# Moving a negated table to ScalarE, GpSimd's index work to the end of its queue, and splitting the last batch of inverse roots

## The chip, the cores and the metric

The kernel runs on one core of one Trainium2 chip. Its time is the device time of one execution in microseconds (us). Five engines work side by side, each in the order of its own queue: PE (TensorE, matrix products), DVE (VectorE), ACT (ScalarE), POOL (GpSimd), and SP (SyncE), which here issues the DMA transfers. An engine that has to wait for another waits at the head of its queue, and whatever stands behind waits with it.

## What is computed

The input x is one sequence of S = 2048 rows of D = 512 numbers in bf16. A row is normalized, filtered in two-dimensional frequency space, and added to x; the sum is normalized again and goes through a feed-forward layer with a squared ReLU (F = 1792).

```python
def _layernorm(x, axis=-1, eps=1e-5):
    m = jnp.mean(x, axis=axis, keepdims=True)
    v = jnp.var(x, axis=axis, keepdims=True)
    return (x - m) / jnp.sqrt(v + eps)

    def _A_ref(x, w_r, w_i):
        B, S, D = x.shape
        X = rfft2(x.astype(jnp.float32), axes=(-2, -1))
        X = X * (w_r + 1j * w_i)
        return irfft2(X, s=(S, D), axes=(-2, -1)).astype(jnp.bfloat16)

    def _B_ref(x, w1, b1, w2, b2):
        h = jnp.einsum("bsd,df->bsf", x, w1) + b1
        r = jnp.where(h > 0, h, 0)
        return jnp.einsum("bsf,fd->bsd", r * r, w2) + b2

    h = x + _A_ref(_layernorm(x), A_w_r, A_w_i)
    return h + _B_ref(_layernorm(h), B_w1, B_b1, B_w2, B_b2)
```

## The kernel before

**Tiling.** The 2048 rows lie as 128 partitions times G = 16 groups: row 16p + g is partition p of group g. The Fourier transforms are chains of matrix products with tables of sines and cosines that the kernel makes itself. Four forward steps matter here.

- First, each group is transformed over its 128 partitions. The table KF (128 x 256) is the same for all groups, but the normalization divides each row by its standard deviation, and a row is a partition of a group; so each group has its own table KR[g] = KF times the row's inverse deviation rs1 (and a constant, WSC). PE multiplies group g of xs by KR[g] (L403, L404). Groups 0 to 9 go in pairs into a PSUM bank `m_p`, groups 10 to 15 in units (10, 11), (12, 13), (14), (15) and in two halves t into banks `s_p`. ACT (t = 0, and all pairs: L419) and DVE (t = 1: L435) cast the results into Bt.
- Second ("stage 2", L502): PE transforms over the 512 columns with the table GF, for the first pair (`pr` 0) and the next in two portions each, and ACT or DVE cast into U (L512).
- Third ("stage 3", L481): PE combines the groups with the table EF, whose third part is the negative of its first (L353, DVE). For the first pair the result goes to AB in two halves, ACT's and DVE's (L540); for the others in one cast of ACT (L579).
- DVE multiplies with the filter W (m, L600) and combines (X, Z, M: L586, L610, L621, L623). For all pairs but the first it also needs the mirrored filter rows, which SP copies in reversed order from a scratch buffer (W<-wx, L280).

The inverse runs back: PE with the table EI (L642 to L647), then GI, then KI. EI[0] and EI[1] are EF[0] and EF[1] transposed by DMA (L440), and EI[2] is the negative of EI[0]. From about 48 us on comes the feed-forward part in chunks of groups, on PE first of all (L902 up, L931 down).

**The inverse deviations.** DVE takes mean and variance of each group (bn_stats L384, bn_aggr L386; groups 3 and 6 on ACT), adds eps for a batch of groups at once (L389), and GpSimd raises the sums to -1/2 in place (L391, called roots below). The batches are groups 0-1, 2-5, 6-9, 10-12 and 13-15. GpSimd then makes the tables KR of groups 0 to 9 (L396), DVE those of 10 to 15.

**Order.** The order on each engine is made on the host when the program is built. Each piece of work is a task with an engine, an estimated duration, tasks or data that it reads, and a priority; the planner `Plan.run` gives each engine at each step the ready task of the lowest priority number (ready: by its own estimates of when the inputs are done). `pin` then nails that order down for each engine. The planner's `reads` and `order` decide only the order: waits between the engines on the chip come from the framework, from the tiles that an instruction really reads and writes.

**Other names.** fiI (L460) is index work of GpSimd, four instructions, from which ACT later makes GI. CN (L456), nm (L463, L465) and GF's scaling (L348) are small DVE work between the tables and stage 3. Where PE is planned to be idle, `warm` (L236) puts in products with zeros.

Of the kernel before, what the change touches and what calls it, by code (L numbers as in the profile page):

```python
# [9 lines left out]
ALU = mybir.AluOpType  # L10
ACT = mybir.ActivationFunctionType
# [22 lines left out]
class Plan:  # L34
# [13 lines left out]
    def add(self, eng, w, fn, reads=(), writes=(), prio=0.0, alloc=None, at=0.0, shared=False, lag=0.0,  # L48
            uses=(), order=()):
        many = isinstance(eng, tuple)  # L50
        ways = dict(zip(eng, w)) if many else {eng: w}
        t = dict(many=many, eng=None, ways=ways, w=0.0, fn=fn, reads=list(reads), writes=list(writes), prio=prio, alloc=alloc, at=at,
                 shared=shared, lag=lag, end=None, order=list(order), n=len(self.tasks))
        self.tasks.append(t)
        for k in t["writes"]:
            self.made.setdefault(k, []).append(t)
        for k in set(t["reads"]) | set(t["writes"]) | set(uses):
            self.use.setdefault(k, []).append(t)
# [82 lines left out]
def kernel(  # L141
# [17 lines left out]
    G = 16  # L159
    NF = F // P  # L160
    ND = D // P
    EPS = 1e-5
    WSC = 2.0 / (S * D)
# [17 lines left out]
    mv1 = persist.tile([P, G, 2], FP32, name="mv1")  # L181
# [14 lines left out]
    KF = fwd.tile([P, 2, P], BF16, name="KF")  # L196
    KR = fwd.tile([P, G, 2, P], BF16, name="KR")
    GF = fwd.tile([P, 2, 2, 256], BF16, name="GF")
    EF = fwd.tile([P, 3, 9, P], BF16, name="EF")
    EI = fwd.tile([P, 3, 9, P], BF16, name="EI")  # L200
# [3 lines left out]
    rs1 = fwd.tile([P, G], FP32, name="rs1")  # L204
# [15 lines left out]
    fiI = tab.tile([P, 4, 256], I32, name="fiI")  # L220
    idxD = tab.tile([P, 256], I32, name="idxD")
# [4 lines left out]
    gp, ve, sc, pe, sy = nc.gpsimd, nc.vector, nc.scalar, nc.tensor, nc.sync  # L226
# [5 lines left out]
    add = plan.add  # L232
# [19 lines left out]
    def sin_of(dst, fi):  # L252
        sc.activation(dst, fi, ACT.Sin, scale=SIN_SCALE)

    def lo(fi):
        return fi.bitcast(I16)[:, ::2]

    def flat(t):
        n = len(t.shape)
        return t if n == 2 else t.rearrange("p a b -> p (a b)") if n == 3 else t.rearrange("p a b c -> p (a b c)")  # L260
# [3 lines left out]
    for c, (a, b) in enumerate(CH):  # L264
        add("SP", 0.45, lambda a=a, b=b: sy.dma_start(xs[:, a:b, :], xv[:, a:b, :]),
            writes=[("x", g) for g in range(a, b)], prio=c, at=0.7, lag=LAND[c])
# [4 lines left out]
    for i in range(2):  # L271
        add("SP", 2.0, lambda i=i: sy.dma_start(wx[i][:].rearrange("k j l -> j k l"),
                                                wv[i].rearrange("k j l -> j k l")[9:16, ::-1, 1:L + 1]),
            writes=[("wx", i)], prio=6 + i, at=1.0, lag=5.0)
    for i in range(2):
        add("SP", 1.0, lambda i=i: (sy.dma_start(W[:, i], wv[i][:, 0:8, 1:L + 1]),
                                        sy.dma_start(W[:, 2 + i, 0], wv[i][:, 8, 1:L + 1])), writes=[("Wn", i)],
            prio=8 + i, at=1.0, lag=6.0)
    for i in range(2):
        add("SP", 1.0, lambda i=i: sy.dma_start(W[:, 2 + i, 1:8], wx[i][:, ::-1]), reads=[("wx", i)], writes=[("Wr", i)],  # L280
            prio=10 + i, lag=6.0)
# [4 lines left out]
    def dve(w, fn, prio, reads=(), writes=(), shared=False, **k):  # L286
        add("DVE", w, fn, reads=reads, writes=writes, prio=prio, shared=shared, **k)

    def act(w, fn, prio, reads=(), writes=(), **k):
        add("ACT", w, fn, reads=reads, writes=writes, prio=prio, **k)  # L290

    def iota(dst, pattern, base, cm):
# [5 lines left out]
         writes=["idxE"])  # L298
# [66 lines left out]

    ON_ACT = (3, 6)
    SQ = 5
    BATCH = ((0, 2), (2, 6), (6, 10), (10, 13), (13, 16))
    KRP = range(10)
    RT = float(1.0 / np.sqrt(D))  # L370
    for bi, (a, b) in enumerate(BATCH):
        z = 10 * bi + 10
        for g in range(a, b):
            if g in ON_ACT:
                act(0.76, lambda g=g: sc.activation(junk[:], xs[:, g, :], ACT.Identity, scale=-RT / D,
                                                    accum_out=nmr[:, g:g + 1]), z - 30, reads=[("x", g)],
                    writes=[("sm", g)])
                act(0.82, lambda g=g: sc.activation(junk[:], xs[:, g, :], ACT.Square, scale=RT, bias=nmr[:, g:g + 1],
                                                    accum_out=mv1[:, g, 1:2]), z - 30, reads=[("x", g), ("sm", g), "mv1z"],
                    writes=[("mv", g)])  # L380
            else:
                def bn(g=g):
                    st = buf(fwd, ("st", g), "st", [P, 6], FP32, 4)
                    ve.bn_stats(st[:], xs[:, g, :])  # L384
                dve(0.63, bn, z, reads=[("x", g)], writes=[("st", g)], alloc=("st", ("st", g)))
                dve(0.12, lambda g=g: ve.bn_aggr(mv1[:, g, :], T["st", g][:]), z - 1, reads=[("st", g), "mv1z"],  # L386
                    writes=[("mv", g)])
        mvs = [("mv", g) for g in range(a, b)]
        dve(0.13, lambda a=a, b=b: ve.tensor_single_scalar(rs1[:, a:b], mv1[:, a:b, 1], EPS, ALU.add), z - 1,  # L389
            reads=mvs, writes=[("va", bi)])  # L390
        pool(0.42 + 0.155 * (b - a), lambda a=a, b=b: gp.tensor_tensor(rs1[:, a:b], rs1[:, a:b], mhalf[:, 0:b - a],  # L391
                                                                     ALU.pow), z - 1, reads=[("va", bi), "mhalf"],
             writes=[("rs", bi)])
        for g in range(a, b):
            e = "POOL" if g in KRP else "DVE"
            add(e, 0.46 if g in KRP else 0.22, lambda g=g, e={"POOL": gp, "DVE": ve}[e]: e.tensor_scalar(  # L396
                flat(KR[:, g]), flat(KF[:]), rs1[:, g:g + 1], WSC, ALU.mult, ALU.mult), prio=z - 5,
                reads=[("rs", bi), "KF"], writes=[("KR", g)], shared=e == "DVE")
    BIG = 10
    UNITS = ((10, 12), (12, 14), (14, 15), (15, 16))  # L400
# [39 lines left out]
        add("SP", 2.5, lambda: sy.dma_start(dst, src, transpose=True), reads=dep, writes=[("EI", i)], prio=prio, lag=4.0)  # L440
    for i in range(2):
        tr_dma(i, EI[:, i], flat(EF[:, i]), [f"EF{i}"], 12 + i)
    EI2 = "DVE"
    add(*((("DVE", 0.46, lambda: ve.tensor_scalar(EI[:, 2], EI[:, 0], -1.0, None, ALU.mult)) if EI2 == "DVE" else
           ("ACT", 1.1, lambda: sc.activation(flat(EI[:, 2]), flat(EI[:, 0]), ACT.Identity, scale=-1.0)))),
        prio=79.0, reads=[("EI", 0)], order=["EF2"], writes=[("EI", 2)])
    tr_dma(3, KI[:], flat(KF[:]), ["KF"], 16)
    for k, (d, s) in ((0, (W1[:], B_w1.rearrange("(c p) f -> p c f", p=P))),
                      (1, (W2[:], B_w2.rearrange("(i p) d -> p i d", p=P))),
# [9 lines left out]
    for lt in range(4):  # L459
        pool(0.48, lambda lt=lt: gp.tensor_scalar(fiI[:, lt], idxD[:], pF[:, 5 + lt % 2:6 + lt % 2],  # L460
                                                  float((QT, HT)[lt // 2]), ALU.mult, ALU.add), 400.0,
             reads=["pF2", "idxD", ("rs", 2 if lt == 0 else 3)], writes=["fiI"])
    dve(0.15, lambda: ve.tensor_scalar(nm1[:], mv1[:, :, 0], -1.0, None, ALU.mult), 190.0,  # L463
        reads=[("mv", g) for g in range(G)], order=["EF2"], writes=["nm0"])
    dve(0.15, lambda: ve.tensor_scalar(nm1[:, 3:7:3], nmr[:, 3:7:3], 1.0 / RT, None, ALU.mult), 190.0,  # L465
# [2 lines left out]
    def mid_tasks():  # L468
        def b1t():
            mm(sg_tile(("b1",))[:, 0:NF], lhsT=b1b[:], rhs=ident[0:NF, 0:NF], start=True, stop=True)  # L470
        add("PE", 0.07, b1t, reads=["b1b", "ident"], order=[("p3", 3)], writes=[("b1",)], prio=141.0, alloc=("sg", ("b1",)))
        act(0.19, lambda: sc.copy(b1f[:], T[("b1",)][:, 0:NF]), 142.0, reads=[("b1",)], writes=["b1f"])
        act(1.07, lambda: sin_of(flat(GI[:]), lo(flat(fiI[:]))), 142.0, reads=["fiI"], order=[("p3", 4)], writes=["GI"])
        act(1.4, lambda: sc.activation(junk[:, 0:1], eps[:], ACT.Sqrt), 0.0, reads=["GI", "eps", ("p4", SQ)], writes=["sqrt"])

# [500 lines left out]
```

## Time and profile before

The median of three runs is 163.07 us (162.92 to 163.09). The profiled execution has a span of 161.7 us and 2907 instructions.

| stretch (us) | PE busy | DVE busy | ACT busy | POOL busy |
|---|---|---|---|---|
| 0 to 16 | 14.54 | 13.96 | 12.58 | 13.54 |
| 16 to 25 | 7.75 | 7.38 | 4.82 | 2.95 |
| 25 to 48 | 21.90 | 22.47 | 21.31 | 0.00 |
| 48 to 161.7 | 110.12 | 78.21 | 61.65 | 16.98 |

The table adds the busy time of each engine in four stretches of the span. Matmuls are pipelined and fillers count, so PE's busy time is not work that has to be done. The rows are to be read with the stages: up to 16 us tables and statistics are made, from 16 to 25 the last tables and the first products of stages 2 and 3, from 25 to 48 the filter and the inverse, and then the feed-forward part. The clock that PE was granted is full in all four (1.00).

In the lines of the profile, `PEld` is PE's loading of the stationary operand; a line of the timeline gives start, duration, engine, line of the kernel, operation, output<-input, shapes, the number of merged instructions, and in brackets the idle time of the engine before it and what ended it. In the answer on waits, a line gives who waited for whom, the sum in us, the number of times and the longest. In the answer on one tile, three numbers with slashes are the shortest, median and longest duration in ns.

### The profile page before, as it was taken

The page shows a single profiled execution, that of the slowest core. Times are in us where ns is not written, and L with a number is a line of the kernel's source. Part 1 is how long each engine was busy: PE and PEld are TensorE (multiplying, and loading weights), DVE is VectorE, ACT ScalarE, POOL GpSimd, SP SyncE. Part 2 cuts the span into 40 slices and gives each one's busy share as a digit, 9 for nine tenths or more (in the row PEclk, how much of TensorE's full clock was granted, in tenths as well). Part 3 has the DMA queues.
Part 4 walks back from the last instruction along what each step waited for, and adds up shares of the span by engine and source line. Part 5 has one row for each costly group of instructions (what it writes and reads, how often), then busy time and mean ns, then how long its engine had stood idle before and what let it go on. Part 6 is the DMA issues. An engine that isn't in the chain of part 4 may idle for free.

```text
span 161.7 us, 2907 instructions
## 1 busy us (share of the span) xinstructions
PE 154.3 (95%) x1037; PEld 92.2 (57%) x1037; DVE 122.0 (75%) x325; ACT 100.4 (62%) x184; POOL 33.5 (21%) x83
## 2 busy tenths in 40 slices
PE   6999889999979899999999999999999999999992
PEld 3477666687658697565644544444544444565461
DVE  6998979999986996879882799993398981385321
ACT  8967647999886798469730779730389830088100
POOL 8789600000000005122140003351002240000000
PEclk9999999999999999999999999999999999999999
DMA  4958999992000001010313000115100122010011
GB/s 141 339 169 235 190 238 232 402 358 74 2 4 0 0 4 34 2 65 4 65 32 97 32 0 4 32 34 130 65 0 6 32 64 66 32 34 4 0 65 32
DMA packets 21017, 13.43 MB, mean 83 GB/s; under 512 B 9738, under 2 KB 19722, under 8 KB 21002
## 3 DMA queue, kind: packets, MB, share of 16 engines
q1 hardware_dynamic: 21002, 13.25, 30.6%
q8 instruction: 8, 0.13, 0.3%
q14 instruction: 7, 0.06, 0.1%
HBM read 8.92 MB, written 3.01 MB: 74 GB/s over the span
## 4 chain that ended last, share of the span: by engine, by line
PE 67%; DVE 18%; DMA 6%; POOL 4%; issue 3%; ACT 0%; DVEq 0%
PE po L931 30%; PE sg L902 20%; PE ph L902 10%; DVE m L600 5%; DMA EI<-EF 4%; DVE Z L610 3%; POOL KR L396 2%; DMA xs<-in_A_x_dram 2%; DVE M L621 2%; DVE X L586 2%; POOL rs L391 2%; DVE st L384 2%; DVE M L623 2%; PE pp L757 1%; PE pp L764 1%
## 5 line engine op out<-in xcount | busy, mean ns | idle before, releaser
L931 PE MATMUL po<-W,act 128*128 128x512 bf16 (+1 forms) x238 | 50.0, 366 | 0.0
L914 ACT ACTIVATE rl<-sg,b1f 128x384 bf16<-128x384 f32 (+2 forms) x46 | 27.3, 602 | 21.8 <-PE sg L902 20.6
L902 PEld LDWEIGHTS <-W 128*128 128x128 bf16 x288 | 26.8, 98 | 19.7 <-issue 0.2
L902 PE MATMUL sg<-UT,W 128*128 128x384 bf16 (+2 forms) x184 | 37.2, 337 | 0.0
L931 PEld LDWEIGHTS <-act 128*128 128x128 bf16 x238 | 23.2, 98 | 24.1
L920 DVE TENSOR_TENSOR act<-rl 128x384 bf16<-128x384 bf16 (+2 forms) x70 | 25.0, 367 | 6.5 <-ACT rl L914 6.0
L940 DVE TENSOR_TENSOR ot<-po,hb 128x512 bf16<-128x512 f32 (+1 forms) x17 | 11.2, 659 | 20.7 <-PE po L931 20.4
L849 POOL TENSOR_SCALAR rs<-ss 128x1 f32<-128x1 f32 x14 | 6.1, 436 | 93.9 <-ACT junk L669 93.9
L902 PE MATMUL ph<-UT,W 128*128 128x512 bf16 (+3 forms) x96 | 19.9, 330 | 0.1
L914 ACT ACTIVATE rl<-ph,b1f 128x512 bf16<-128x512 f32 (+2 forms) x23 | 13.9, 602 | 10.0 <-PE ph L902 9.4
L785 DVE TENSOR_TENSOR hs<-pp,xs 128x512 bf16<-128x512 f32 x14 | 9.7, 690 | 2.3 <-PE pp L757 1.3
L669 ACT ACTIVATE junk<-hs,nm 128x512 bf16<-128x512 bf16 x14 | 10.0, 713 | 0.1
L481 PE MATMUL m_p<-U,EF 128*128 128x512 bf16 (+1 forms) x46 | 9.5, 337 | 0.0
L780 DVE TENSOR_TENSOR R<-q 128x127 bf16<-128x127 f32 x40 | 9.4, 283 | 0.0
L384 DVE BATCH_NORM_STATS2 st<-xs 128x6 f32<-128x512 bf16 x14 | 9.0, 670 | 0.3 <-DMA xs<-in_A_x_dram 0.3
L789 DVE TENSOR_TENSOR hb<-hs,b2b 128x512 f32<-128x512 bf16 x14 | 9.1, 682 | 0.0
L579 ACT CAST AB<-m_p 128x1024 bf16<-128x1024 f32 x7 | 7.1, 1018 | 3.0 <-PE m_p L481 2.9
L851 POOL TENSOR_TENSOR rs<-rs,mhalf 128x1 f32<-128x1 f32 x14 | 8.0, 571 | 1.2
L360 PE MATMUL s_fa<-fz 128*128 128x512 bf16 x30 | 7.9, 428 | 0.0
L747 DVE TENSOR_TENSOR q<-pp,od 128x256 f32<-128x256 f32 x20 | 7.6, 415 | 0.0
L502 PEld LDWEIGHTS <-Bt 128*128 128x128 bf16 x64 | 6.1, 97 | 1.5 <-DVE Bt L435 0.2
L481 PEld LDWEIGHTS <-EF 128*128 128x128 bf16 x52 | 5.1, 97 | 3.4 <-issue 0.9
(158 smaller groups left out, 226.9 us busy)
## 6 DMA issues: line engine op xcount, KB each, us to landing
W<-in_B_w_dram SPq DMA_DIRECT2D x2, 1792.0 KB, 10.3
out_dram<-ot SPq DMA_DIRECT2D x15, 128.0 KB, 1.8
xs<-in_A_x_dram SPq DMA_DIRECT2D x4, 256.0 KB, 3.9
xs<-in_A_x_dram SPq DMA_DIRECT2D x2, 512.0 KB, 6.6
W<-wx SPq DMA_DIRECT2D x2, 448.0 KB
W<-in_A_w_r_dram SPq DMA_DIRECT2D x1, 512.0 KB, 8.7
W<-in_A_w_i_dram SPq DMA_DIRECT2D x1, 512.0 KB, 6.9
wx<-in_A_w_r_dram SPq DMA_DIRECT2D x1, 448.0 KB
```

Of the source, the lines that this page charges most:

```text
L384: ve.bn_stats(st[:], xs[:, g, :])
L481: mm(o.rearrange("p (j i e) -> p j i e", e=2, i=RUN), lhsT=w, rhs=U[:, q, s].rearrange("p (j e i) -> p j i e", e=2, i=RUN), **k)
L600: ve.tensor_tensor(m[:, u:u + n].rearrange("p u i r c -> p u i (r c)"), X, w, ALU.mult)
L669: sc.activation(junk[:], src, ACT.Square, bias=nm1[:, g:g + 1], accum_out=ss2[:, g:g + 1])
L780: ve.tensor_tensor(o, x, y, (ALU.add, ALU.subtract, ALU.subtract, ALU.add)[k])
L785: dve(0.66, lambda g=g: ve.tensor_tensor(hs[:, g, :], T["p6", g][:], xs[:, g, :], ALU.add), z, reads=[("p6", g)], writes=[("hs", g)])
L789: add(("DVE", "POOL")[HBP], (0.62, 1.3)[HBP], lambda g=g: (ve, gp)[HBP].tensor_tensor(hb[:, g, :], hs[:, g, :], b2b[:], ALU.add), prio=lat ...
L902: mm(p[:, P * i0:P * i1], lhsT=W1[:, d, bass.ts(f, P)], rhs=T["UT", c][:, i0:i1, d, :], start=(d == 0), stop=(d == ND - 1))
L914: sc.activation(r[:, 0:P * n], T["ph", c, f][:, 0:P * n], ACT.Relu, bias=b1f[:, f:f + 1], scale=1.0)
L920: ve.tensor_tensor(t[:, f, 0:P * n], r[:, 0:P * n], r[:, 0:P * n], ALU.mult)
L931: mm(p[:, cs], lhsT=T["act", c][:, f, bass.ts(i, P)], rhs=W2[:, f, cs], start=(f == 0), stop=(f == NF - 1))
L940: ve.tensor_tensor(o[:, cs], T["po", g, h][:, cs], hb[:, g, cs], ALU.add)
```

## The change

Five edits in one stretch of the kernel.

1. The negated table EI[2] is made by ACT instead of DVE, in ACT's queue behind its half of the cast of the first pair (`("X", 0, 0)`). It is for taking the wait for the DMA out of DVE's queue.
2. The table KR[9] is made by ACT instead of GpSimd. It is for shortening GpSimd's queue before the roots of groups 10 and up.
3. The last two batches of roots, 3 and 3 groups, become three of 3, 2 and 1.
4. The constant WSC moves from each table's multiplication into the eps addition (times WSC to the -2, before the power -1/2), so that ACT, which multiplies with one scale per row, can make a table too; L396 has one multiplication left of two. DVE's tables get a planner's priority of 55.
5. The planner holds fiI behind the last table, `("KR", G - 1)`, instead of behind roots.

```diff
-    BATCH = ((0, 2), (2, 6), (6, 10), (10, 13), (13, 16))
-    KRP = range(10)
+    BATCH = ((0, 2), (2, 6), (6, 10), (10, 13), (13, 15), (15, 16))
+    KRP = range(9)
+    KRA = (9,)
...
-        z = 10 * bi + 10
+        z = 10 * min(bi, 4) + 10
...
-        dve(0.13, lambda a=a, b=b: ve.tensor_single_scalar(rs1[:, a:b], mv1[:, a:b, 1], EPS, ALU.add), z - 1,
+        dve(0.13, lambda a=a, b=b: ve.tensor_scalar(rs1[:, a:b], mv1[:, a:b, 1], EPS, float(WSC ** -2), ALU.add, ALU.mult), z - 1,
             reads=mvs, writes=[("va", bi)])
...
             e = "POOL" if g in KRP else "DVE"
+            if g in KRA:
+                act(0.4, lambda g=g: sc.activation(flat(KR[:, g]), flat(KF[:]), ACT.Identity, scale=rs1[:, g:g + 1]), z - 5,
+                    reads=[("rs", bi), "KF"], writes=[("KR", g)])
+                continue
             add(e, 0.46 if g in KRP else 0.22, lambda g=g, e={"POOL": gp, "DVE": ve}[e]: e.tensor_scalar(
-                flat(KR[:, g]), flat(KF[:]), rs1[:, g:g + 1], WSC, ALU.mult, ALU.mult), prio=z - 5,
+                flat(KR[:, g]), flat(KF[:]), rs1[:, g:g + 1], None, ALU.mult), prio=z - 5 if g in KRP else 55,
                 reads=[("rs", bi), "KF"], writes=[("KR", g)], shared=e == "DVE")
...
-    EI2 = "DVE"
-    add(*((("DVE", 0.46, lambda: ve.tensor_scalar(EI[:, 2], EI[:, 0], -1.0, None, ALU.mult)) if EI2 == "DVE" else
-           ("ACT", 1.1, lambda: sc.activation(flat(EI[:, 2]), flat(EI[:, 0]), ACT.Identity, scale=-1.0)))),
-        prio=79.0, reads=[("EI", 0)], order=["EF2"], writes=[("EI", 2)])
...
-             reads=["pF2", "idxD", ("rs", 2 if lt == 0 else 3)], writes=["fiI"])
+             reads=["pF2", "idxD", ("KR", G - 1)], writes=["fiI"])
...
+        act(1.1, lambda: sc.activation(flat(EI[:, 2]), flat(EI[:, 0]), ACT.Identity, scale=-1.0), 83.0, reads=[("EI", 0)],
+            order=["EF2", ("X", 0, 0)], writes=[("EI", 2)])
```

## The prediction

> **What bounds the kernel now.** I read the page's shares and slices first, then the chain of waits for the stretch that the change touches, then the timelines of each engine there, then the waits.
>
> The page says that no engine bounds the whole kernel:
>
> ```profile
> PE 154.3 (95%) x1037; PEld 92.2 (57%) x1037; DVE 122.0 (75%) x325; ACT 100.4 (62%) x184; POOL 33.5 (21%) x83
> PE 67%; DVE 18%; DMA 6%; POOL 4%; issue 3%; ACT 0%; DVEq 0%
> ```
>
> PE's 95% includes filler matmuls. The second line, the chain that ended last, is two thirds PE, all of it after 48 us (the feed-forward part). Before that the chain runs through POOL, DMA and DVE. The change edits only work between 13 and 24 us, so that stretch of the chain decides:
>
> ```profile
> 12.51 0.99 POOL rs L391
> 13.50 0.09 issue
> 13.59 1.85 POOL KR L396 x4
> 15.45 0.45 POOL rs L391
> 15.89 6.34 DMA EI<-EF
> 22.26 0.46 DVE EI L444
> 22.72 0.08 DVE nm L463
> 22.80 0.59 DVE U L512
> ```
>
> Two things bind. GpSimd makes tables and roots without a pause until 15.9. Then the chain stands on the transposing copy of EI, because DVE has the negation (L444) at the head of its queue and stands still until the copy lands. The 6.34 us is the copy's own age; what DVE loses is in its timeline and in the waits:
>
> ```profile
> 16.32 2.25 DVE L396 TENSOR_SCALAR KR<-KF,rs 128x256 bf16<-128x256 bf16 x6 [0.76 <-POOL rs L391]
> 20.87 0.25 DVE L456 TENSOR_SCALAR CN<-EF 128x384 bf16<-128x384 bf16 x1
> 22.26 0.46 DVE L444 TENSOR_SCALAR EI<-EI 128x1152 bf16<-128x1152 bf16 x1 [1.13 <-DMA EI<-EF]
> 22.71 0.68 DVE L512 CAST U<-s_p 128x512 bf16<-128x512 f32 x1
> 23.38 0.68 DVE L512 CAST U<-m_p 128x512 bf16<-128x512 f32 x1
> 24.08 0.69 DVE L540 CAST AB<-s_p 128x512 bf16<-128x512 f32 x1
> PE s_p L481 <- DVE U L512: 0.6, 1, 0.6
> ACT AB L579 <- PE m_p L481: 1.9, 1, 1.9
> ```
>
> DVE has no other gap from 16.32 to 24. Behind L444 stand the two U casts, for which PE waits (0.6 us); and ACT has 1.9 us free before its AB cast. GpSimd's timeline beside it, and the table group on DVE:
>
> ```profile
> 15.41 1.70 POOL L391 TENSOR_TENSOR rs<-rs,mhalf 128x3 f32<-128x3 f32 x2
> 17.10 1.85 POOL L460 TENSOR_SCALAR fiI<-idxD,pF 128x256 int32<-128x256 int32 x4
> L396 DVE TENSOR_SCALAR KR<-KF,rs x6: 281/401/544, 16.3 to 18.0; 128x256 bf16<-128x256 bf16 x6
> ```
>
> The six DVE tables are two kinds: the first three (16.32 to 17.0, GpSimd in roots) took 0.28 us and follow each other every 0.20; the last three (17.14 to 18.57, beside the fiI index work) took 0.52 to 0.54 and follow each other every 0.43 to 0.46, which is GpSimd's own beat (0.46).
>
> **What the Trainium skill says.** "SBUF — State Buffer", Who interferes with whom: a DVE tensor_scalar in a two-port mode and a GpSimd instruction exclude each other for the whole instruction. The trace agrees for fiI (0.54 against 0.28 us), and shows no such loss beside the roots. "ScalarE: Activation LUTs", What ACT_TABLE_LOAD costs: an ACTIVATE costs 186 ns + 0.833 ns per element, 93 ns more for each per-row operand. The trace agrees: 1.147 us for 1152 elements (EF), 1.255 with a per-row scale (fiE). "GPSIMD Engine Reference", 3.1: with up to two operations per element the loop is bound by its ports; so one multiply less at L396 should gain nothing. No row of before has the one-operation form.
>
> **The change part by part.** Times are starts on the chip, before -> after. The compiled order of both kernels shows that after DVE's EI edit the instructions are the same on all engines to the end, and SP's queue is unchanged.
>
> 1. Table 9 goes from GpSimd to ACT. GpSimd's last table starts at 14.97 and takes 0.48: its queue is shorter by 0.46. On ACT it costs 0.186 + 0.093 + 256 x 0.000833 = 0.49 us (the skill's price; trace floor: the 0.37 us cast of 256 elements). ACT ends a cast at 14.39 and starts the next at 15.22, so 14.30 to 14.79 is free, and PE needs table 9 only at 15.5: nothing on the path.
>
> 2. Roots. Batch 3 starts 15.41 -> 14.97 (its input is there at 13.8), takes 0.87, ends 15.84. Batches of 2 and 1 follow: 0.73 us (the two-root row at 7.48; its bounds are the one-root and three-root rows, 0.57 and 0.86, whose middle is 0.72) and 0.57 (the one-root mean of L851): 16.55 and 17.10. Three take 2.13 us where two took 1.70, so the last root ends where it did (17.11 -> 17.10), but the first five tables no longer wait for it. The one added DVE add (0.1 us, 15.5) lies in DVE's 0.76 us wait.
>
> 3. DVE tables. 10, 11, 12 at 15.87, 16.07, 16.27 (from 16.32: -0.45). 13 and 14 after the second root: 16.58, 16.78, now clear of fiI. 15 after the third root: 17.13. Here I do not take the change's word for it: fiI "behind the last scaled table" is a rule of the planner alone. Its four instructions carry no wait in the compiled order, nor did they before, and share no data with the tables; GpSimd will start them at 17.10, right after the last root. So table 15 still collides and holds 0.44. The next DVE instruction (GF) starts 18.48 -> 17.57: -0.91, of which 0.45 is the earlier start and 0.46 the collisions saved less the waits for roots. If fiI does wait, -1.15.
>
> 4. To stage 2. The Bt casts on DVE keep their beat: 17.67, 18.27, 18.87, 19.25. Does PE supply them? A table reaches PE 0.05 after DVE, and each group of a half takes PE 0.22: from 16.20 on, groups 10 and 11 are through at 17.24, 12 and 13 at 18.12; group 14's second half waits for the bank of the first DVE cast, as before (PE's 0.53 us wait at 19.31), so 18.40; the last half starts 18.84 and is ready at 19.22, in time for the cast at 19.25. ACT's halves of that stage can start at 17.04, since its five big casts before them did not move (16.13 for the last, as PE delivers). The last DVE cast ends 20.59 -> 19.68: -0.91. EF and CN follow; fiI is over at 18.95, so they do not collide.
>
> 5. EI off DVE. Without L444, CN ends at 20.2 and the first U cast waits only for PE's stage 2, which ended at 21.58 -> 20.67: cast at 20.71 -> done 21.39. PE ends its other stage-2 and first stage-3 product at 21.8; the second product starts there: 23.45 -> 21.82 = -1.63. So the EI edit adds 0.72, not 1.13 + 0.46: the rest was PE's own work. The AB cast on DVE comes 0.63 after: 24.08 -> 22.45.
>
> 6. EI on ACT: 186 ns + 1152 x 0.833 ns = 1.15 us. It waits for the copy (landing 22.23, set by DMA alone) and its place behind the AB cast (22.93 -> 22.02, done 22.6): about 22.5 to 23.67. Queued behind it is ACT's L579, whose input PE ends at 25.34 - 1.63 = 23.7. Just hidden; even 1.25 us would cost under 0.1, and DVE's X needs that cast only 0.3 later.
>
> 7. Limits that do not move. DVE's second spectrum product (27.47 -> 25.84) needs the reversed filter copies W<-wx. Their landing is not in the printed views; the trace's completion counts put the last packet at 25.68. Slack 0.16 us: this caps the gain at some 1.75. PE's inverse stage (29.49 -> 27.86) needs the second EI copy (26.70). GI needs fiI (18.95 as before). W1 and W2 landed at 32.3 and 38.9, used after 54 and 60.
>
> From 25 to 48 us DVE, ACT and PE are each 90% or more busy on one another's output, all of it shifted; after 48 us PE runs the same instructions. So the shift reaches the end: 163.07 - 1.63 = 161.44, say **161.45 us**.
>
> **Rivals.**
> A, forecast: 161.45 (61%).
> B, the reversed copies hold DVE: the sequencer's wait in DVE's timeline ended at 26.49 at the latest, so in the worst reading the product starts 26.5: gain 0.97, 162.1. For it: slack is only 0.16. Against: completion counts. 18%.
> C, only one half arrives (fiI also slowing EF and CN, or ACT's negation late because EI lands 0.7 later): gain 0.72 to 0.91, about 162.25. 9%.
> D, the cap: one multiply on GpSimd is cheaper, or fiI waits: gain up to 1.75, 161.3. 5%.
> E, nothing arrives within 0.2%: 2%, 163.0.
> F, slower: ACT becomes the bound, table 9 (0.49) and negation (1.06 net) both on the path and 0.46 of GpSimd back: +1.1, 164.1. ACT is 90% full from 25 to 48, which speaks for it; its gaps at 14.4 and 23.5 speak against. 5%.
>
> **Numbers.** 161.2 holds the cap with the measurement's spread (0.17); 162.2 takes in B and most of C. Left out: some of C, E, F, about 15%. Faster 0.93, same 0.02, slower 0.05.
>
> **What would show it.** KR on DVE starts near 15.87, with four or five of six at 0.28 and the last at 0.5; fiI at 17.1; no DMA wait on DVE at 22; EI on ACT about 22.5, 1.15 us; AB on ACT 23.75; DVE's m near 23.06; the 2048-wide m at 25.84, or held by a DMA (then B). Wrong if PE's clock drops in that stretch (three filler matmuls fewer), or ACT's L579 is late.

## The result: slower, and the profile after

| | median (us) | lowest to highest |
|---|---|---|
| before | 163.08 | 162.92 to 163.27 |
| after | 165.71 | 165.70 to 165.74 |

The ratio is 1.0163 (95% interval 1.0150 to 1.0176): 2.6 us slower, where 161.45 had been forecast and 162.2 was the top of the range. The time is 1.77 us longer than the span in every profiled execution here, so spans can be compared as times can. But the profiled execution of before, whose span is 161.7, took 163.51 us, 0.43 above its median; differences between profiles are therefore that much more favourable to a changed kernel than differences between medians. Between the two profiles the kernel lost 2.2 us.

The page of after, in the lines of busy time by engine and of the chain that ended last:

```profile
PE 154.7 (94%) x1025; PEld 92.2 (56%) x1034; DVE 121.3 (74%) x325; ACT 101.9 (62%) x186; POOL 37.2 (23%) x83
PE 81%; POOL 7%; DVE 6%; DMA 2%; ACT 1%; issue 1%; DVEq 0%
```

GpSimd is busy for 3.7 us more than before (33.5), although it has one table less to make. The chain of waits has lost its DMA part (6% to 2%), as the change meant, but GpSimd's part has grown from 4% to 7%. The same chain in order of time (start, duration, what) says where:

```profile
8.29 1.84 POOL KR L401 x2
10.14 1.02 POOL rs L392
11.25 3.62 POOL KR L401 x4
14.88 1.01 POOL rs L392
15.97 2.74 POOL KR L401 x3
18.75 0.27 PE m_p L408
```

Nine tables now stand on the chain from end to end, each about 0.92 us long. In before's chain four tables took 1.85 us; here two do. The groups that touch the tile KR give the single duration (shortest/median/longest in ns, first and last start in us), the first line in before, the others in after:

```profile
L396 POOL TENSOR_SCALAR KR<-KF,rs x10: 477/482/487, 8.3 to 15.0; 128x256 bf16<-128x256 bf16 x10
L401 POOL TENSOR_SCALAR KR<-KF,rs x9: 922/922/938, 8.3 to 17.8; 128x256 bf16<-128x256 bf16 x9
L401 DVE TENSOR_SCALAR KR<-KF,rs x6: 279/284/394, 19.6 to 20.9; 128x256 bf16<-128x256 bf16 x6
L398 ACT ACTIVATE KR<-KF,rs x1: 510/510/510, 16.5 to 16.5; 128x256 bf16<-128x256 bf16 x1
```

GpSimd's instruction is the same in tile, type and per-row scale; what is gone is the second multiplication, and the time has nearly doubled. On DVE the same edit did nothing to the duration (shortest 281 before, 279 after).

DVE's timeline shows how this travels (start, duration of the group, instruction, and in brackets the idle time before it and who ended it):

```profile
19.57 1.70 DVE L401 TENSOR_SCALAR KR<-KF,rs 128x256 bf16<-128x256 bf16 x6 [4.00 <-POOL rs L392]
...
24.38 0.69 DVE L515 CAST U<-s_p 128x512 bf16<-128x512 f32 x1 [0.21 <-PE s_p L505]
26.12 0.69 DVE L543 CAST AB<-s_p 128x512 bf16<-128x512 f32 x1 [0.18 <-PE s_p L484]
```

DVE stands still for 4.0 us until GpSimd has made the tables and then the roots that lie behind them in its queue. Its first table starts at 19.57, 3.25 us later than before (16.32). The wait for the transposing copy of EI is gone, but there was nothing left for this to save: DVE now comes to that place in its queue at 24 us, and in after the copy (issued at 16.1 us, 6.8 us to landing) was there at 22.9. PE stands still for the same tables, in six pieces (waits between 13 and 28 us: sum, times, longest):

```profile
PE m_p L408 <- POOL KR L401: 2.4, 6, 0.9
```

The chain leaves GpSimd after the last table for PE (18.75), and not by way of the roots and DVE. PE takes up DVE's first table at 19.9 us, right behind its products of groups 8 and 9 and four with zeros, so the two ways are late alike.

### The profile page after: what moved, and what is told of

Its sections match the earlier page's. It is cut to its first block, busy times and chain, and to the rows that moved or that the text cites. A ratio compares the mean times of both kernels' runs of the same rounds, so it can differ in the third digit from the quotient of the medians.

```text
span 163.9 us, 2895 instructions
## 1 busy us (share of the span) xinstructions
PE 154.7 (94%) x1025; PEld 92.2 (56%) x1034; DVE 121.3 (74%) x325; ACT 101.9 (62%) x186; POOL 37.2 (23%) x83
## 4 chain that ended last, share of the span: by engine, by line
PE 81%; POOL 7%; DVE 6%; DMA 2%; ACT 1%; issue 1%; DVEq 0%
PE po L934 29%; PE sg L905 20%; PE ph L905 10%; POOL KR L401 5%; PE m_p L484 5%; PE m_p L505 4%; DMA xs<-in_A_x_dram 2%; POOL rs L392 2%; PE m_p L650 2%; PE pp L760 1%; PE pp L767 1%; PE s_p L408 1%; DVE Z L613 1%; PE s_p L409 1%; DVE M L624 1%
## 5 line engine op out<-in xcount | busy, mean ns | idle before, releaser
L934 PE MATMUL po<-W,act 128*128 128x512 bf16 (+1 forms) x229 | 48.7, 366 | 0.5
L917 ACT ACTIVATE rl<-sg,b1f 128x384 bf16<-128x384 f32 (+2 forms) x46 | 27.3, 601 | 21.9 <-PE sg L905 20.6
L905 PE MATMUL ph<-UT,W 128*128 128x512 bf16 (+3 forms) x96 | 19.9, 330 | 0.1
L424 ACT CAST Bt<-m_p 128x1024 bf16<-128x1024 f32 x5 | 5.1, 1012 | 5.7 <-PE m_p L409 5.7
L360 PE MATMUL s_fa<-fz 128*128 128x512 bf16 x30 | 8.4, 450 | 0.0
L401 POOL TENSOR_SCALAR KR<-KF,rs 128x256 bf16<-128x256 bf16 x9 | 8.2, 926 | 0.3
L582 ACT CAST AB<-m_p 128x1024 bf16<-128x1024 f32 x7 | 7.1, 1019 | 1.6 <-PE m_p L484 1.6
```

What stands on the lines that cost most here:

```text
L905: mm(p[:, P * i0:P * i1], lhsT=W1[:, d, bass.ts(f, P)], rhs=T["UT", c][:, i0:i1, d, :], start=(d == 0), stop=(d == ND - 1))
L917: sc.activation(r[:, 0:P * n], T["ph", c, f][:, 0:P * n], ACT.Relu, bias=b1f[:, f:f + 1], scale=1.0)
L934: mm(p[:, cs], lhsT=T["act", c][:, f, bass.ts(i, P)], rhs=W2[:, f, cs], start=(f == 0), stop=(f == NF - 1))
```

## The experiments

**One multiplication or two.** Two kernels put the second multiplication back (times 1.0, which changes nothing in the value) or take it away alone.

e1_two_op, from after:

```diff
-                flat(KR[:, g]), flat(KF[:]), rs1[:, g:g + 1], None, ALU.mult), prio=z - 5 if g in KRP else 55,
+                flat(KR[:, g]), flat(KF[:]), rs1[:, g:g + 1], *((1.0, ALU.mult, ALU.mult) if g in KRP else (None, ALU.mult))), prio=z - 5 if g in KRP else 55,
```

> The whole change, but GpSimd's tables multiply twice again (by the root and by 1.0). Theory 1, the one-operation form is what costs GpSimd 0.92 us a table instead of 0.48, and the rest of the forecast holds: tables back at 0.48, first DVE table near 15.9 us, time 161.45 (161.2 to 161.9). Theory 2, something else in the change slows GpSimd's tables (split roots, DVE or ACT beside it): they stay near 0.92 and the time near 165.7.

Measured: 162.27 us, ratio to before 0.9943 (0.9919 to 0.9967). The group of the nine tables on GpSimd:

```profile
L401 POOL TENSOR_SCALAR KR<-KF,rs x9: 473/479/501, 8.3 to 14.5; 128x256 bf16<-128x256 bf16 x9
```

DVE's timeline behind them:

```profile
15.83 1.70 DVE L401 TENSOR_SCALAR KR<-KF,rs 128x256 bf16<-128x256 bf16 x6 [0.30 <-POOL rs L392]
17.44 0.19 DVE L348 TENSOR_SCALAR GF<-GF 128x4 bf16<-128x4 bf16 x1
...
22.37 0.69 DVE L543 CAST AB<-s_p 128x512 bf16<-128x512 f32 x1 [0.18 <-PE s_p L484]
22.98 1.28 DVE L603 TENSOR_TENSOR m<-AB,W 128x1024 bf16<-128x1024 bf16 x2
...
25.91 1.22 DVE L603 TENSOR_TENSOR m<-X,W 128x2048 bf16<-128x2048 bf16 x1
```

With a multiplication more the kernel is 3.4 us faster than after. The tables take 0.479 us again, and the five starts shown lie within 0.13 us of those in the prediction (15.87, 17.57, 22.45, 23.06, 25.84). The span is 1.57 us shorter than before's profile, where 1.63 had been forecast. The median is nevertheless above the 161.2 to 161.9 expected here, and a little above the top of the forecast's range (162.2); the end of the account below comes back to this.

e2_before_one_op, from before: WSC goes into the eps addition, as in the change, and L396 keeps one multiplication. Nothing else of the change is in it.

```diff
-        dve(0.13, lambda a=a, b=b: ve.tensor_single_scalar(rs1[:, a:b], mv1[:, a:b, 1], EPS, ALU.add), z - 1,
+        dve(0.13, lambda a=a, b=b: ve.tensor_scalar(rs1[:, a:b], mv1[:, a:b, 1], EPS, float(WSC ** -2), ALU.add, ALU.mult), z - 1,
...
-                flat(KR[:, g]), flat(KF[:]), rs1[:, g:g + 1], WSC, ALU.mult, ALU.mult), prio=z - 5,
+                flat(KR[:, g]), flat(KF[:]), rs1[:, g:g + 1], None, ALU.mult), prio=z - 5,
```

> The kernel before with one edit only: WSC goes into the eps addition, and the tables multiply once. Theory 1: ten GpSimd tables at 0.92; the last follows 4.1 us later, the first DVE table about 20.4; the DMA wait on DVE (0.72 us of the path) vanishes under that; time 163.1 + 4.1 - 0.7 = 166.5. Theory 2: tables at 0.48, time 163.1.

Measured: 167.09 us, ratio 1.0234 (1.0207 to 1.0260). In DVE's timeline:

```profile
20.50 2.25 DVE L396 TENSOR_SCALAR KR<-KF,rs 128x256 bf16<-128x256 bf16 x6 [4.89 <-POOL rs L391]
...
25.21 0.45 DVE L444 TENSOR_SCALAR EI<-EI 128x1152 bf16<-128x1152 bf16 x1
```

There are ten long tables instead of nine, and DVE begins 4.2 us late. The time is 0.6 us more than expected. The negation of EI, here still on DVE, has no DMA wait before it at 25.21. So the one edit makes the kernel slower by about what the whole change costs plus what the rest of it gains: 1.0234 x 0.9943 = 1.0176, against 1.0163 measured for the whole.

**The instruction by itself.** e3_probe appends 14 instructions to the end of before, for GpSimd alone and after the last output: two copies and then the table's instruction in several forms, on 256 and on 1024 elements. Its time is longer only by these. Here `pin_` and `pr` are scratch tiles in bf16 (prs and prb in the profile), `pf` is one in fp32 (prf), `sca` is one number per row, and n is the number of elements.

```diff
...
+    for n in (256, 1024):
+        gp.tensor_scalar(pr[:, 0:n], pin_[:, 0:n], sca, 1.0, ALU.mult, ALU.mult)
+        gp.tensor_scalar(pr[:, 0:n], pin_[:, 0:n], sca, None, ALU.mult)
+        gp.tensor_scalar(pr[:, 0:n], pin_[:, 0:n], sca, 0.0, ALU.mult, ALU.add)
+        gp.tensor_scalar(pr[:, 0:n], pin_[:, 0:n], 2.0, None, ALU.mult)
+        gp.tensor_scalar(pf[:, 0:n], pin_[:, 0:n], sca, None, ALU.mult)
+        gp.tensor_scalar(pf[:, 0:n], pin_[:, 0:n], sca, 1.0, ALU.mult, ALU.mult)
```

> The kernel before, with fourteen GpSimd instructions appended behind the last output, where GpSimd is alone; the time is longer by them and tells nothing. Two copies, then six forms of scaling at 256 and at 1024 elements: (a) per-row scale times 1.0, (b) per-row scale alone, (c) per-row scale plus 0.0, (d) constant alone, (e) per-row scale alone into fp32, (f) per-row scale times 1.0 into fp32. Theory 1: a and c 0.48 us at 256, b 0.92, that is a cost per element, so b is near 3.3 us at 1024 and a near 1.1. Theory 2: all alike at 256.

GpSimd's timeline at the end, L954 being scale and times 1.0, L955 scale alone, L956 scale and plus 0.0, L957 a constant alone:

```profile
160.13 0.48 POOL L954 TENSOR_SCALAR prb<-prs,rs 128x256 bf16<-128x256 bf16 x1
160.71 0.93 POOL L955 TENSOR_SCALAR prb<-prs,rs 128x256 bf16<-128x256 bf16 x1
161.73 0.48 POOL L956 TENSOR_SCALAR prb<-prs,rs 128x256 bf16<-128x256 bf16 x1
162.30 0.85 POOL L957 TENSOR_SCALAR prb<-prs 128x256 bf16<-128x256 bf16 x1
...
164.59 1.12 POOL L954 TENSOR_SCALAR prb<-prs,rs 128x1024 bf16<-128x1024 bf16 x1
165.80 2.84 POOL L955 TENSOR_SCALAR prb<-prs,rs 128x1024 bf16<-128x1024 bf16 x1
```

From 256 to 1024 elements the form with two operations grows by 1.118 - 0.477 = 0.641 us, 0.83 ns per element; the form with one by 2.842 - 0.930 = 1.912 us, 2.49 ns per element, three times as much. What is left at no elements is about the same for both (an estimate from these figures: 0.26 and 0.29 us). Which second operation it is does not matter (1.0 or plus 0.0), nor does the output's type (the same two durations into fp32); a constant alone in place of the per-row scale is nearly as slow. So it is the missing second operation, whatever the neighbours in the kernel do. Why GpSimd runs it so, no run here shows.

**The parts of the rest.** e4_ei_only is before with nothing of the change but the negated EI on ACT (the diff's edit 1).

```diff
-    EI2 = "DVE"
-    add(*((("DVE", 0.46, lambda: ve.tensor_scalar(EI[:, 2], EI[:, 0], -1.0, None, ALU.mult)) if EI2 == "DVE" else
...
+        act(1.1, lambda: sc.activation(flat(EI[:, 2]), flat(EI[:, 0]), ACT.Identity, scale=-1.0), 83.0, reads=[("EI", 0)],
+            order=["EF2", ("X", 0, 0)], writes=[("EI", 2)])
```

> The kernel before with one edit only: the negated inverse table on ACT. The forecast's step 5: second stage-3 product 0.72 us earlier, time 162.35. Rival, ACT becomes the bound: L579 later than 24.7 us and time 163.1 or more.

Measured: median 162.89 us, ratio 0.9954 (0.9932 to 0.9975). The ratio is worth 0.75 us, close to the 0.72 expected, the median only 0.3, because the eleven executions form two groups, five from 161.89 to 162.41 and six from 162.89 to 163.11. The profile is one of the second group; DVE's first X is at 26.08 in it, 0.60 earlier than in before. The cast L579 starts at 25.03, later than the 24.7 named as the sign of the rival; but ACT has waited 0.48 us for PE just before it, so ACT is not the bound.

e8_tables_only is the other half: e1 with the negation back on DVE, by the lines of before (edit 1 of the diff taken back).

```diff
+    EI2 = "DVE"
+    add(*((("DVE", 0.46, lambda: ve.tensor_scalar(EI[:, 2], EI[:, 0], -1.0, None, ALU.mult)) if EI2 == "DVE" else
...
-        act(1.1, lambda: sc.activation(flat(EI[:, 2]), flat(EI[:, 0]), ACT.Identity, scale=-1.0), 83.0, reads=[("EI", 0)],
...
```

> As e1, but the negated table EI is on DVE again, behind CN: the tables', roots' and index half of the change alone. The forecast: DVE still waits for EI's landing near 22.2 us, so the 0.9 us won before it is lost there; time 163.0, within 0.2 of before. Rival: the half is worth 0.9 by itself, 162.2.

Measured: 162.91 us, ratio 0.9992 (0.9980 to 1.0004). DVE's timeline:

```profile
15.83 1.70 DVE L401 TENSOR_SCALAR KR<-KF,rs 128x256 bf16<-128x256 bf16 x6 [0.30 <-POOL rs L392]
17.44 0.19 DVE L348 TENSOR_SCALAR GF<-GF 128x4 bf16<-128x4 bf16 x1
...
21.38 0.46 DVE L449 TENSOR_SCALAR EI<-EI 128x1152 bf16<-128x1152 bf16 x1 [1.02 <-DMA EI<-EF]
```

GF starts as in e1, 1.04 us earlier than before, and DVE then loses 1.02 us at the negation. The shorter roots and tables are worth nothing as long as DVE waits for the copy; the two parts have to come together.

**Why e1 varies.** e1's executions lie from 161.94 to 162.83 us, while after's lie within 0.04. Three kernels look for the cause in late copies (rivals B and C): e5_no_wx lets all products but the first pair's read filter rows that the reversed copy does not write, e6_no_ei negates EF[0], which no DMA makes, and e7_neither does both. They start from e1.

```diff
-            w = W[:, 2 * u:2 * u + 2 * n, pr].unsqueeze(2).to_broadcast([P, 2 * n, 2, 256])
+            w = (W[:, 0:1, pr] if pr else W[:, 2 * u:2 * u + 2 * n, pr]).unsqueeze(2).to_broadcast([P, 2 * n, 2, 256])
```

```diff
-        act(1.1, lambda: sc.activation(flat(EI[:, 2]), flat(EI[:, 0]), ACT.Identity, scale=-1.0), 83.0, reads=[("EI", 0)],
+        act(1.1, lambda: sc.activation(flat(EI[:, 2]), flat(EF[:, 0]), ACT.Identity, scale=-1.0), 83.0, reads=[("EI", 0)],
```

> As e1 (whole change, two multiplications on GpSimd), but DVE's filter products of pairs 1 to 7 read a natural filter row four times over and so never wait for the reversed copies W<-wx; the copies still run. It leaves out the mirrored half of the filter. e1 had a span 1.54 us shorter in its profile, but its timed runs spread from 161.9 to 162.8. Theory B: in the timed runs the reversed copies often land late and hold DVE; then this gives 161.5, with a spread under 0.2. Rival: another copy or none is at fault; then 161.9 to 162.8 as e1.

> As e1, but ACT negates EF instead of its transposed copy, so that it doesn't wait for the transposing DMA (a wrong table, same size). Theory C: the EI copy lands late in the timed runs and holds ACT's negation and the AB cast behind it; then 161.5 with a spread under 0.2. Theory B: 161.9 to 162.8 as e1.

> Both edits, of e5 and of e6: neither the reversed copies nor the EI copy can hold DVE or ACT before PE's inverse stage. If one of B and C, or both, is the cause of e1's spread, 161.5 with a spread under 0.2. If it is still spread, the cause is another transfer (the filter's natural rows, the input) or none.

Measured: 162.09 us (161.95 to 163.14), 162.16 (161.96 to 163.11) and 162.09 (161.55 to 163.00); ratios 0.9953 (0.9933 to 0.9974), 0.9962 (0.9938 to 0.9985) and 0.9946 (0.9930 to 0.9963). The spread stays with both copies taken away, so the copies are not its cause. But in e7 the six executions from 162.69 up are just those with a mean granted PE clock of 0.997 or 0.998; the nine at 1.0 end at 162.29. The profile of e5 caught such an execution (163.08 us, clock 0.998). The mean itself is a clue and no more, for in e5 the granted clock falls below 1.00 only behind 160 us, where PE has nothing left to do. PE's timeline in e1:

```profile
1.96 7.70 PE L360 MATMUL s_fa<-fz 128*128 128x512 bf16 x30
9.49 0.27 PE L408 MATMUL m_p<-KR,xs 128*128 128x256 bf16 x1
```

And in e5:

```profile
1.96 9.20 PE L360 MATMUL s_fa<-fz 128*128 128x512 bf16 x30
10.99 0.27 PE L408 MATMUL m_p<-KR,xs 128*128 128x256 bf16 x1
```

L360 is 30 products with zeros that keep PE busy from the start on, ahead of the first product with a table. They take 1.5 us longer in the second. In the trace one of them starts every 0.43 us at first and every 0.22 us later, and the change of pace comes at 4.1 us in e1 and at 7.1 us in e5. (The granted clock does not show this: it reads 1.00 from the start, in the table of before as well, although before's products too kept the slow pace up to 4.5 us.) Table 0 is ready at 8.8 us in both. So the useful work starts 0.7 us late in one execution and 2.2 us in the other. The Trainium skill, "TensorE: Matmul & The Clock Gate", Part 1, says that PE starts at half its clock and that the moment at which it rises differs between runs of one kernel; the traces agree, with a pace that doubles at 4.1 to 7.1 us over the fourteen profiled executions. The times go with it: the profiles of e7, e6 and e5 have the change at 4.1, 4.9 and 7.1 us and took 161.95, 162.08 and 163.08 us. e9_fewer_fill tests it: e1 with 24 of these products.

```diff
-        fill(("fa", i), 4 if i < 6 else 3, -1.0, at=1.3 + 0.9 * i)
+        fill(("fa", i), 3, -1.0, at=1.3 + 0.9 * i)
```

> As e1, with 24 instead of 30 filler products of zeros in front of PE's first table product. In the profiles so far the full PE clock came at 4.1 to 7.1 us after the start, the fillers ended at 9.6 to 11.2 with it, the first table has been ready at 8.8, and the span of e1 to e7 grew with that moment. Theory D, PE enters the stretch with a backlog of fillers and binds it in the executions whose clock comes late, whatever the tables do: six fillers less (2.6 us cold, 1.3 us warm) take the backlog away; 161.9 in nearly all runs, spread under 0.3. Rival: the fillers are hidden and the spread is of another cause; 161.9 to 162.8 as e1.

Measured: 161.96 us (161.78 to 161.98), ratio 0.9933 (0.9920 to 0.9946). The spread of the five executions is 0.2 us where e1's was 0.9, and the one with a clock of 0.997 took 161.98. (e10 below, with 24 too, has a spread of 0.9 again, so this holds for e1's variation and not for every cause of one.) PE's timeline:

```profile
1.96 6.66 PE L360 MATMUL s_fa<-fz 128*128 128x512 bf16 x24
8.85 0.27 PE L408 MATMUL m_p<-KR,xs 128*128 128x256 bf16 x1 [0.23 <-POOL KR L401]
```

PE now waits for the table, not the table for PE. The same edit in before, e11_before_fewer_fill:

> The kernel before with 24 instead of 30 fillers. Theory D: in before the landing of EI's copy holds DVE until 22.2, so that an earlier PE wins nothing: 163.0, within 0.2 of before. Rival: the fillers alone are what can be won, 162.2.

Measured: 163.04 us, ratio 1.0001 (0.9986 to 1.0015). DVE's timeline in its profiled execution (163.06):

```profile
21.77 0.46 DVE L444 TENSOR_SCALAR EI<-EI 128x1152 bf16<-128x1152 bf16 x1 [0.67 <-DMA EI<-EF]
```

DVE's wait for the copy of EI is still there, and takes up a late PE. In after, PE's own wait for GpSimd's long tables (2.4 us above) would do the same: after's times lie within 0.04 us, and those of e2, with the same long tables, within 0.02. No run tests this apart.

**The index work that does not wait.** The planner's rule puts fiI behind the last table, but fiI started at 20.71 in after, right behind the last root. e10_fii_late, from e9, makes it wait for a thing that it really reads: DVE's copy pF2 goes behind CN.

```diff
-    dve(0.13, lambda: ve.tensor_copy(pF[:, 5:7], pI[:, 5:7]), 0.65, reads=["p2"], writes=["pF2"], shared=True)
+    dve(0.13, lambda: ve.tensor_copy(pF[:, 5:7], pI[:, 5:7]), 77.0, reads=["p2"], writes=["pF2"], order=["CN"])
```

> As e9, and the small DVE copy that fiI reads (pF2) stands behind CN, so that GpSimd's fiI really has to wait for DVE. Forecast's step 3: fiI starts near 20.2 instead of 17.1, the sixth table on DVE falls from 0.39 us to 0.28 and GF starts 0.2 earlier; 0.2 us off the time if DVE binds there. Rival: PE binds there; same time as e9.

Measured: 161.89 us (161.18 to 162.04), ratio 0.9920 (0.9904 to 0.9937), the lowest median of all, though its interval overlaps that of e9. In its profiled execution (162.04) fiI starts at 20.24, as expected. DVE's timeline:

```profile
15.76 1.59 DVE L401 TENSOR_SCALAR KR<-KF,rs 128x256 bf16<-128x256 bf16 x6 [0.30 <-POOL rs L392]
17.26 0.17 DVE L348 TENSOR_SCALAR GF<-GF 128x4 bf16<-128x4 bf16 x1
...
20.56 0.69 DVE L515 CAST U<-s_p 128x512 bf16<-128x512 f32 x1
...
26.01 1.23 DVE L603 TENSOR_TENSOR m<-X,W 128x2048 bf16<-128x2048 bf16 x1 [0.20 <-DMA W<-wx]
```

The same cast in e9:

```profile
20.64 0.69 DVE L515 CAST U<-s_p 128x512 bf16<-128x512 f32 x1 [0.21 <-PE s_p L505]
```

GF is 0.19 us earlier than in e9, but the first U cast only 0.08, because in e9 DVE had waited there for PE. And the tables before it start 0.08 earlier too (15.76 for 15.84), as the small copy no longer stands early in DVE's queue. So up to this cast the rival is right: PE binds. Behind it DVE waits for the reversed filter rows, as step 7 of the prediction feared, and the 0.08 is lost in this execution. Why others go down to 161.18 is not shown.

The same copy edit on top of e4 is e12_ei_fii:

> As e4 (before, with the negated table on ACT), and pF2 behind CN, so that GpSimd's index work can't run beside DVE's last three tables. e4's timed runs fall into two groups, about 161.9 to 162.4 and 162.9, and its profile was of the second. Theory E: in the first group DVE happens to take the shared port before fiI; then this kernel always has three tables at 0.28 us, GF near 17.7 instead of 18.46, and no run with full clock at 162.9: 161.9 to 162.2. Rival: the collision isn't the cause; two groups as in e4, both 0.7 lower or unmoved.

Measured: 162.36 us, ratio 0.9952 (0.9936 to 0.9969), above the 161.9 to 162.2 expected. In its DVE timeline:

```profile
16.24 1.50 DVE L396 TENSOR_SCALAR KR<-KF,rs 128x256 bf16<-128x256 bf16 x6 [0.76 <-POOL rs L391]
17.66 0.17 DVE L348 TENSOR_SCALAR GF<-GF 128x4 bf16<-128x4 bf16 x1
```

The six tables take 1.50 us where before's took 2.25, and GF comes at 17.66 where before it came at 18.48. None of the seven executions is at 162.9; four are at 162.34 to 162.36, the others at 162.49, 162.74 and 163.10. That fits the collision between fiI and three DVE tables as the cost in e4's slower group, and the chain of e4's profile does run through these three tables:

```profile
17.12 1.43 DVE KR L396 x3
```

It does not prove it. The profiled execution of e12 took 162.74, only 0.17 less than that of e4, and its chain runs through PE's products with zeros instead (the pace changed at 6.2 us in both):

```profile
2.16 8.49 PE s_fa L360 x30
```

Why some executions of e4 reach 161.9 stays open.

## Why the prediction was wrong

**The step that failed** is the price of a table with one multiplication: "with up to two operations per element the loop is bound by its ports; so one multiply less at L396 should gain nothing. No row of before has the one-operation form." It was priced at the 0.48 us of the two-operation form and measures 0.92. The Trainium skill, "GPSIMD Engine Reference", 3.1, says 1.03 cycles per element for up to two operations, so it makes no difference between one and two. The probe does: 0.83 ns per element with two, 2.49 with one, and the measurement decides. The prediction saw that the form was in no row, and still gave it only a lower side: rival D let it be cheaper, and none let it be dearer. The tables were on the chain all the time: the prediction itself says that GpSimd makes tables and roots without a pause until 15.9.

The term, sized anew: 9 x (0.922 - 0.479) = 4.0 us more on GpSimd. Of this, 0.3 us go into waits for roots' inputs that GpSimd had before. The other 3.7 are the difference between DVE's first table as forecast (15.87) and as measured (19.57), and they are still 3.7 at the AB cast (22.45 and 26.12). Against the forecast gain of 1.63 that makes 2.1 us slower; the profiled spans differ by 2.2, the medians by 2.6.

The other steps, from after and, with the tables' price restored, from e1:

- Step 1, ACT's table: 0.51 us for a forecast 0.49, and nothing waited for it. That GpSimd's queue becomes 0.46 shorter holds in e1 (last table at 14.5 for 14.97).
- Step 2, roots of 3, 2 and 1: DVE's first table at 15.83 in e1, forecast 15.87.
- Step 3, fiI does not wait for the last table: right. GpSimd's timeline of after has it behind the roots without a gap, and the sixth table takes 0.394 us beside it:

```profile
18.66 2.18 POOL L392 TENSOR_TENSOR rs<-rs,mhalf 128x3 f32<-128x3 f32 x3
20.71 1.84 POOL L461 TENSOR_SCALAR fiI<-idxD,pF 128x256 int32<-128x256 int32 x4
```

- Steps 4 and 5: first U cast at 20.63 in e1 for a forecast 20.71, AB at 22.37 for 22.45. e8 shows the two halves' dependence on each other directly. In e9, where the first products with zeros no longer stand in the way, the chain goes from GpSimd's seventh table (13.57) straight to PE and stays on it until 21.9. So PE, not DVE's earlier tables, sets the time of the U cast there. 0.6 us of that stretch are again products with zeros, put in by `warm`; whether they cost anything no run tests.
- Step 6, the negation on ACT just hidden: 1.167 us for 1.15, which agrees with the price of the Trainium skill, "ScalarE: Activation LUTs", What ACT_TABLE_LOAD costs. ACT's timeline in e1:

```profile
22.42 1.17 ACT L474 ACTIVATE EI<-EI 128x1152 bf16<-128x1152 bf16 x1
24.07 1.01 ACT L582 CAST AB<-m_p 128x1024 bf16<-128x1024 f32 x1 [0.48 <-PE m_p L484]
```

ACT waits for PE afterwards, so it is not the bound (rival F fell; that it had named "slower" was luck, since its reason did not hold). L582 comes 0.3 later than the forecast 23.75. PE waits 0.24 us for ACT's cast L543 ahead of the product that L582 reads; that wait was missed. DVE's X is 0.07 later than the forecast.

- Step 7, the cap: it exists, as e10 shows, but it is not a fixed one. There the reversed rows hold DVE until 26.01, where step 7 put the landing at 25.68; e10's fastest execution, 161.18, gains 1.89 on 163.07, more than the cap of 1.75.

With the tables' price restored the forecast would still have missed: e1's median is 162.27, 0.8 us above 161.45. Two things that were not in the prediction make up about that much.

The first is the base. The gain of 1.63 was read from a profiled execution of 163.51 us and taken off the median, 163.07. From its own execution it gives 163.51 - 1.63 = 161.88, and e1's profiled execution took 161.94. The chain of before stands on EI's copy, and in the profiled execution this landed late. DVE's negation starts at 22.26 there, at 21.77 in e11's profile (163.06 us) and at 21.38 in e8's (162.64), and each time the kernel's time is 141.3 us more than this start; so the copy's landing sets the time in all three. Step 6 took the landing (22.23) as "set by DMA alone", thus as fixed; over the fourteen profiles it lies between 21.1 and 22.9. In e11's execution, which took about as long as the median of before, DVE loses 0.67 us to it and not 1.13.

The second is PE's start. e1's profiled execution is 0.33 below its own median; a late change of PE's pace costs e1 up to 0.9 us, while in before DVE's wait hides it, as far as e11 tells. The prediction noted that PE's 95% includes filler, and did not ask when the first table product starts (9.68 in before, with table 0 ready at 8.8).

## What to carry to other kernels

An operation that no row of the profile shows is not priced by its neighbour with one operation more: give it both sides, and if it stands in a queue that the chain runs through, multiply it by its count and put the bad side into the range. Removing arithmetic from an instruction can make it slower, so an edit that only tidies a constant away is measured alone before it goes in with others. Where PE is kept busy with zeros ahead of the first product, count them for the execution whose clock rises late, and see that none of them stands before ready work. A gain read from a profile is taken off the time of that profiled execution; if this lies off the median, look for what was late in it.

## What the runs showed of the hardware

- GpSimd's tensor_scalar with one operation (bf16 in) takes 0.93 us for 128 x 256 and 2.84 for 128 x 1024; with a second operation that changes nothing (times 1.0, plus 0.0) 0.48 and 1.12. DVE shows no such difference (0.28 us in both forms).
- PE's full pace (128 x 512 products every 0.22 us instead of 0.43) began between 4.1 and 7.1 us after the start, from execution to execution of nearly the same program; with 24 instead of 30 filler products the spread of e1's times was 0.2 us for 0.9.
- The transposing copy of EI (128 x 1152 bf16) landed at 21.1 to 22.9 us over the fourteen profiles.
- DVE's table takes 0.52 to 0.54 us beside GpSimd's index work (before) and 0.28 to 0.29 without it (e10, e12). The Trainium skill states this exclusion in "SBUF — State Buffer", Who interferes with whom, and the trace agrees. Beside GpSimd's roots there is no such loss (0.28 in before).
